# A long convolution followed by a token-mixing layer: GpSimd copies of the input ahead of the first transform's weight loads

## The chip, the cores and the metric

The kernel runs on one core of one Trainium2 chip. The metric is the device time of one execution in microseconds. The engines are named as in the profile: PE is TensorE (PEld its weight loads), DVE is VectorE, ACT is ScalarE, POOL is GpSimd, SP is SyncE, the last of which only issues transfers here.

## The reference

`x` is 8 x 5696 x 128 (batch, token, channel), `h` is 5696 x 128. Two layers follow each other.

```python
# 1: causal long convolution along the tokens, by transforms of twice the length
Xf = np.fft.rfft(x, n=2 * S, axis=1);  Hf = np.fft.rfft(h, n=2 * S, axis=0)
x  = np.fft.irfft(Xf * Hf[None], n=2 * S, axis=1)[:, :S, :]
# 2: phase-aware mixing of the tokens
theta = x @ w_theta                                  # 128 x 128
zr, zi = x * np.cos(theta), x * np.sin(theta)
y = einsum('ts,bsd->btd', w_tok_r, zr) + einsum('ts,bsd->btd', w_tok_i, zi)   # 5696 x 5696 each
u = x + y
out = u + np.maximum(u @ w_ch, 0.0)
```

## The kernel before

The work falls into a transform stage (the first 440 us or so), a stage that computes the phases and writes `zr` and `zi`, and the mixing (two passes of one-level Strassen products over the 5696 x 5696 weights), which takes the rest. The change touches the transform stage alone.

The length 11392 is split as 178 x 64 (`N1` x `N2`). The channels are treated in halves of 64 (`HD`), the batches in pairs, so that there are eight groups `(bp, dh)`: pair `bp`, half `dh`. A group passes four steps:

- **Stage A** (`stage_a`, L185 to L202): the transform of length 178 over the token blocks. The tokens of one batch lie as 89 rows (partitions) of 64; the tile `x16` holds `[89 rows, 2 batches, 64 tokens, 128 channels]` in f16. For each channel one matmul takes as its weights the 2 x 64 columns of that channel and as its moving operand the table `f1_t` of 180 columns. The columns of one channel are 128 elements apart in `x16`, 256 bytes. Four channels make a chunk, in one PSUM tile; 16 chunks make a group. ACT copies each chunk into `a_` (L201). The weights are named by

```python
x16 = x16s[bp].rearrange("p b n d -> p (b n) d")
steps, a_st = stage_a(lambda q: x16[:NB, :, dh * HD + q])
```

- **Stage B** (`stage_b`, `f2`): the transform of length 64 with the twiddles in the weights (L212), ACT's copy out of PSUM (L310), and DVE's two products with the filter's transform, which was computed first and stored in HBM (L312, both inputs in SBUF). Each group's stage B ends with 12 further matmuls (L218), whose output nobody reads.
- **Stage C** (`stage_c`): the way back over 64 points, 16 chunks of 16 matmuls (L328, L329), drained by DVE (L336) and for four of the chunks by ACT (L333, L334).
- **Stage D** (`stage_d`): the way back over 178 points (L351), drained by ACT (L354) and stored in `yt_hbm`.

The order is written out by the function `woven`, which merges lists of steps by given shares of the time. Stage A of group g + 1 is woven into stage C of group g: over the first 35% where g is the first half of a pair (`dh == 0`), over the first 55% otherwise. Stage B of group g + 1 is then woven with stage D of group g. A scheduler beneath the kernel places the instructions on each engine's queue; each queue is worked in order. All transform stages take their PSUM tiles from one ring of four (`psum`).

`x16` has one buffer. `load_x` (L130, sixteen transfers issued by POOL) refills it for the next pair when stage A of the second half has read it. POOL also builds the tables of sines at the beginning: each needs an iota (L150) and a product (L152) by POOL, then work by DVE and ACT. The table `w_table` (used by L212) comes in six parts, `r_table` and `s_table` are woven with stage A of group 0, the three parts of `e_table` with its stage B.

The filter `h` passes the same stage A and `f2` once before, from its own tile `h16`.

Of the kernel before, what the change touches and what calls it, by code (L numbers as in the profile page):

```python
# [12 lines left out]
F16 = mybir.dt.float16  # L13
# [9 lines left out]
def kernel(  # L23
# [10 lines left out]
    nc = tc.nc  # L34
    B, S, D = x.shape
    assert D == 128
    P = 128
# [39 lines left out]
    N2 = 64  # L77
    N1 = NF // N2
    NB = S // N2
    K1 = N1 // 2 + 1  # L80
    CK = 8
    HD = D // 2
# [14 lines left out]
    def psum():  # L97
        return fp.tile([P, 2, 512], F32, tag="ps", name="ps")

    conv, setup, xa, xin, pha = (ExitStack() for _ in range(5))  # L100

    def pool(name, bufs, stack, **kw):
        return stack.enter_context(tc.tile_pool(name=name, bufs=bufs, **kw))

    fa = pool("fft_a", 1, xa)
    fh = pool("fft_h", 4, xa)
    fx = pool("fft_x", 1, xin)
    NE, WB, BT = 9, 6 * 4 * CJ * 64, 7 * 1024
    keep = pool("keep", 1, ctx, side="right")
    fc = pool("fft_c", 1, conv, side="right")  # L110
# [7 lines left out]
    h16 = s1.tile([P, 2, N2, HD], F16)  # L118
# [5 lines left out]
    def load_x(bp):  # L124
        x16 = fx.tile([P, 2, N2, D], F16, tag="x16", name="x16")
        for e in range(2):
            src = x[2 * bp + e]
            for n0 in range(0, N2, 16):
                for p0, p1 in ((0, 80), (80, NB)):
                    nc.gpsimd.dma_start(  # L130
                        x16[p0:p1, e, n0:n0 + 16, :].rearrange("p n d -> p (n d)"),
                        bass.AP(tensor=src.tensor, offset=src.offset + (p0 * N2 + n0) * D,
                                ap=[[N2 * D, p1 - p0], [1, 16 * D]]))
        return x16
# [34 lines left out]
    f1_t = fc.tile([P, 2 * K1], F16)  # L169
# [7 lines left out]
    def w_table(k0):  # L177
        t, k = turns_of([[1, 15], [N1, N2]], k0, lane[:, 0:1], P, NF)
        t3, k3 = (z.rearrange("p (k n) -> p k n", n=N2) for z in (t, k))
        sine(w_t2[:, k0:k0 + 15, :N2], t3, 1)  # L180
        cosine(w_t2[:, k0:k0 + 15, N2:2 * N2], t3, k3)
        nc.vector.tensor_scalar(w_t2[:, k0:k0 + 15, 2 * N2:], w_t2[:, k0:k0 + 15, :N2],
                                -1.0, None, op0=mult)

    def stage_a(lhs, both=False):  # L185

        st = {}

        def chunk(q):
            if q == 0:  # L190
                st["a"] = fa.tile([P, 2 * K1, HD], F16, tag="a", name="a_")
            ps = psum()
            for i in range(4):
                nc.tensor.matmul(ps[:, i // 2, (i % 2) * 2 * K1:(i % 2 + 1) * 2 * K1], lhs(q + i), f1_t[:NB],  # L194
                                 start=True, stop=True)
            a_out = st["a"][:, :, q:q + 4].rearrange("p k (a q) -> p k a q", a=2)
            a_in = ps[:, :, :4 * K1].rearrange("p a (q k) -> p k a q", q=2)
            if both and q % 8:
                nc.vector.tensor_copy(a_out, a_in)
            else:  # L200
                nc.scalar.activation(a_out, a_in, AF.Copy)  # L201
        return [lambda q=q: chunk(q) for q in range(0, HD, 4)], st  # L202
# [19 lines left out]
    def woven(*lists):  # L222

        lists = [l if isinstance(l, tuple) else (l, 0.0, 1.0) for l in lists]
        steps = [(w0 + (i + 0.5) / len(l) * (w1 - w0), n, f)
                 for n, (l, w0, w1) in enumerate(lists) for i, f in enumerate(l)]
        for _, _, f in sorted(steps, key=lambda s: s[:2]):
            f()
# [2 lines left out]
        w_table(k0)  # L231
    nc.vector.tensor_copy(h16[:NB], u_t[:NB, :N2 * D].rearrange("p (n h d) -> p h n d", h=2, d=HD))
    x16s = {0: load_x(0)}
    steps, a_h = stage_a(lambda q: h16[:NB].rearrange("p h n d -> p (h n) d")[:, :, q], True)
    woven(steps, [lambda k0=k0: w_table(k0) for k0 in range(45, K1, 15)])

    hst = [t[:, :6 * D * CK].rearrange("p (c h d k) -> p c h d k", c=6, h=2, k=CK) for t in (u_t, v_t)]
# [56 lines left out]
    def stage_b(a_st, dh):  # L294

        hs_of = {}

        def load(c):
            if c >= NCK:
                return  # L300
            hs = hs_of[c] = fh.tile([P, 2, HD * CK], F16, tag="hs", name="hs")
            for e in range(2):
                nc.sync.dma_start(hs[64 * e:64 * e + 64], hf_hbm[dh, c])

        def chunk(c):
            c0, ck = CHK[c]
            hv = hs_of[c].rearrange("p r (d k) -> p r d k", k=CK)
            ps = f2(a_st, c)
            xs = fs.tile([P, 2, HD, CK], F16, tag="xs", name="xs")
            nc.scalar.activation(xs[:, :, :, :ck], ps, AF.Copy)  # L310
            for r in range(2):
                nc.vector.tensor_tensor(  # L312
                    uv[r][:, :, :, c0:c0 + ck], xs[:, :, :, :ck],
                    hv[:, r:r + 1, :, :ck].to_broadcast([P, 2, HD, ck]), op=mult)
            load(c + LEAD)
        return [lambda c=c: load(c) for c in range(LEAD)], [lambda c=c: chunk(c) for c in range(NCK)]
# [54 lines left out]
    def front(g):  # L371
        if g >= len(groups):
            return [], [], []
        bp, dh = groups[g]
        x16 = x16s[bp].rearrange("p b n d -> p (b n) d")
        steps, a_st = stage_a(lambda q: x16[:NB, :, dh * HD + q])
        return (steps, *stage_b(a_st, dh))

    a0, load0, b0 = front(0)
    woven(a0, [lambda: r_table(0, r_u), lambda: r_table(1, r_v), s_table] + load0)  # L380
    woven(b0, [lambda n0=n0: e_table(n0) for n0 in range(0, EN, 11)])
# [220 lines left out]
    for g, (bp, dh) in enumerate(groups):  # L602
        st = {}
        last = g + 1 == len(groups)
        a_, load_, b_ = front(g + 1)
        if last:
            for _ in range(3):
                steps0.pop(0)()
        now = [with_load(steps0.pop(0), n < 6) for n in range(9)] if last else []
        c_ = stage_c(st, last)  # L610
        if dh == 0 and bp + 1 < B // 2:
            def next_x(bp=bp):
                x16s[bp + 1] = load_x(bp + 1)
            a_ = a_ + [next_x]
        woven((c_, 0.06 if a_ else 0.0, 1.0), (a_, 0.0, 0.35 if dh == 0 else 0.55), now, load_)
        if g + 2 == len(groups):
            xin.close()
            open_phases()
            load_ya0()
        now = [steps0.pop(0) for _ in range(5)] if last else []  # L620
        woven(b_, (stage_d(st, bp, dh, load_ya1 if last else None), 0.0, 1.1 if b_ else 1.0), now)
        if g + 2 == len(groups):
            load_ya1()
            open_ring()
# [56 lines left out]
    bp = cp = wlp = ybp = None  # L681
# [232 lines left out]
    for i, (k, p, tt, j0, s0, nj) in enumerate(stretches):  # L914
# [38 lines left out]
        if tt is None:  # L953
            if p:
                aside(True, False)
            if first_of_pair:
                ps = [mps.tile([P, 512], F32, tag=f"m{q}", name=f"m{q}") for q in ((M1, M7) if p else (M3, M4))]
# [3 lines left out]
            for j in range(nj):  # L961
                jj = j0 + s0 + j
                for r in range(2):
                    b = [x[:, r, :] for x in bts[jj]]
# [182 lines left out]
```

## Time and profile before

| | |
|---|---|
| time, median of 3 runs | 2110.66 us (2108.34 to 2111.68) |
| the profiled execution | span 2116.2 us, 41712 instructions |
| PE matmuls, weight loads | busy 2008.1 us (95%), 1117.7 us (53%) |
| DVE, ACT, POOL | 1598.3 us (76%), 673.9 us (32%), 907.6 us (43%) |
| the chain that ended last | PE 68%, of it L1084 (mixing) 61% of the span |
| granted PE clock, mean | 0.979; 0.70 from 50 to 100 us |

No time of the profiled execution is given but its span, which is 0.26% over the median of the runs; numbers of the profile are set against the span.

A row of the groups names line, engine, operation, output and inputs, shapes and count, then the busy time and the mean of one; behind the second bar stands the idle time of the engine just before these instructions and who ended most of it. A row of the timeline begins with the start and the length in us and merges instructions of the same kind that follow each other. The durations of PE overlap, since matmuls and loads are pipelined; what a matmul costs in a run of them is the distance from start to start.

### The profile page before, as it was taken

How to read it: one execution, taken by the hardware profiler on the slowest of the kernel's cores; microseconds unless marked ns; L12 is line 12 of the kernel's file. 1: busy time of each engine (PE TensorE's matmuls, PEld its weight loads, DVE VectorE, ACT ScalarE, POOL GpSimd, SP SyncE). 2: the span in 40 equal slices, each digit the busy share in tenths (PEclk: the TensorE clock that was granted, in tenths of full speed). 3: DMA queues.
4: the chain of work that ended last, by engine and by line, in shares of the span. 5: the costliest groups of instructions: out<-in, count | busy, mean ns of one | idle time of the engine just before them, and what ended most of it. 6: DMA issues, size and time to landing. Idle time of an engine off the chain costs nothing.

```text
span 2116.2 us, 41712 instructions
## 1 busy us (share of the span) xinstructions
PE 2008.1 (95%) x15873; PEld 1117.7 (53%) x15873; DVE 1598.3 (76%) x2884; ACT 673.9 (32%) x997; POOL 907.6 (43%) x1662
## 2 busy tenths in 40 slices
PE   4888999778999999999999999999999999999998
PEld 3788888654444444444444444444444444444444
DVE  7767776777778888888886755877777777776867
ACT  5778877774332333332310000111111111111111
POOL 5301010227444536354556543445454444545450
PEclk8799999999999999999999999999999999999999
DMA  6457474889989989898999879878888787979693
GB/s 140 98 130 170 117 180 127 216 245 243 178 153 179 176 176 168 170 176 173 174 165 156 142 137 296 128 117 147 140 143 145 134 153 128 156 127 157 124 156 90
DMA packets 408265, 334.97 MB, mean 158 GB/s; under 512 B 85927, under 2 KB 358439, under 8 KB 407079
## 3 DMA queue, kind: packets, MB, share of 16 engines
q0 software_dynamic: 225952, 156.72, 52.5%
q1 hardware_dynamic: 176128, 164.05, 27.3%
q10 hardware_dynamic: 5984, 11.54, 1.6%
q8 instruction: 124, 2.03, 0.4%
q14 instruction: 77, 0.63, 0.1%
HBM read 377.11 MB, written 92.49 MB: 222 GB/s over the span
## 4 chain that ended last, share of the span: by engine, by line
PE 68%; DMA 3%; DVE 3%; POOL 1%; issue 1%; ACT 0%; DVEq 0%; SPq 0%; POOLq 0%; ACTq 0%
PE m L1084 61%; PE m L1005 2%; DMA ring<-in_moe_w_tok_r_dram 1%; DMA b<-z_hbm 1%; POOL ring L509 1%; PE v L801 1%; PE utp L794 1%; DVE c L1091 1%; PE m L1088 1%; DVE b L655 1%; DVE wt L714 1%; DMA ring<-in_moe_w_tok_i_dram 0%; PE theta_ps L396 0%; PE tpz L742 0%; PE m L968 0%
## 5 line engine op out<-in xcount | busy, mean ns | idle before, releaser
L509 POOL DMA_DIRECT2D ring<-in_moe_w_tok_i_dram x720 | 387.9, 546 | 666.7 <-DVE wt L714 587.7
L714 DVE STREAM_TRANSPOSE wt<-ring 128x384 f32<-128x384 f32 (+2 forms) x720 | 360.5, 527 | 123.2 <-PE m L1084 71.3
L509 POOL DMA_DIRECT2D ring<-in_moe_w_tok_r_dram x720 | 386.4, 546 | 149.3 <-DVE wt L714 86.4
L1084 PE MATMUL m<-b,wt 128*128 128x512 bf16 x1640 | 388.3, 379 | 2.0 <-DVE wt L714 1.7
L1084 PEld LDWEIGHTS <-wt 128*128 128x128 bf16 x1804 | 175.8, 98 | 217.6 <-DVE wt L714 6.2
L1091 DVE TENSOR_TENSOR c<-c,m 128x512 f32<-128x512 f32 x412 | 266.9, 674 | 0.4 <-PE m L1084 0.4
L796 ACT ACTIVATE ring<-utp 128x512 bf16<-128x512 bf16 (+1 forms) x86 | 50.9, 592 | 586.2 <-PE utp L794 586.2
L328 PE MATMUL ps<-r_u,u_t 128*128 128x128 f16 x1024 | 128.6, 226 | 10.8 <-ACT red L419 5.6
L329 PE MATMUL ps<-r_v,v_t 128*128 128x128 f16 x1024 | 127.7, 226 | 0.4
L791 ACT ACTIVATE ub<-c 128x512 bf16<-128x512 f32 (+1 forms) x90 | 56.3, 628 | 215.0 <-DMA ring<-in_moe_w_tok_r_dram 123.8
L1005 PE MATMUL m<-b,wt 128*128 128x512 bf16 x480 | 112.9, 385 | 9.1 <-DVE wt L714 4.4
L130 POOL DMA_DIRECT2D x<-in_x_dram x64 | 33.9, 536 | 189.3 <-PE ps L194 177.8
L328 PEld LDWEIGHTS <-u_t 128*128 128x128 f16 x1024 | 104.1, 102 | 9.6 <-DVE u_t L312 6.2
L329 PEld LDWEIGHTS <-v_t 128*128 128x128 f16 x1024 | 103.4, 101 | 5.7 <-issue 3.2
L310 ACT ACTIVATE xs<-ps 128x1024 f16<-128x1024 f32 x96 | 95.9, 1023 | 15.1 <-DVE v_t L312 7.9
L312 DVE TENSOR_TENSOR u_t<-xs,hs 128x1024 f16<-128x1024 f16 x96 | 68.8, 716 | 32.1 <-ACT xs L310 19.7
L1005 PEld LDWEIGHTS <-wt 128*128 128x128 bf16 x528 | 50.8, 99 | 70.8 <-issue 8.7
L194 PE MATMUL ps<-f_t,x 89*128 89x180 f16 x512 | 77.2, 299 | 5.6 <-ACT xs L310 3.9
L212 PEld LDWEIGHTS <-w_t 64*128 64x128 f16 x3240 | 61.2, 102 | 34.8 <-issue 21.7
L398 ACT ACTIVATE red<-theta_ps,magic 128x512 f32<-128x512 f32 (+1 forms) x46 | 31.6, 687 | 133.7 <-PE theta_ps L396 116.0
L194 PEld LDWEIGHTS <-x 89*128 89x128 f16 x512 | 70.3, 241 | 6.6 <-issue 5.9
L744 ACT ACTIVATE ring<-tpz 128x512 bf16<-128x512 bf16 (+1 forms) x46 | 27.5, 597 | 132.6 <-PE tpz L742 108.9
(2914 smaller groups left out, 3916.7 us busy)
## 6 DMA issues: line engine op xcount, KB each, us to landing
ring<-in_moe_w_tok_r_dram POOLq DMA_DIRECT2D x352, 96.0 KB, 4.4
ring<-in_moe_w_tok_i_dram POOLq DMA_DIRECT2D x352, 96.0 KB, 5.0
ring<-in_moe_w_tok_r_dram POOLq DMA_DIRECT2D x352, 80.0 KB, 4.5
ring<-in_moe_w_tok_i_dram POOLq DMA_DIRECT2D x352, 80.0 KB, 3.9
hs<-hf_hbm SPq DMA_DIRECT2D x192, 128.0 KB, 3.2
cp_hbm<-c SPq DMA_DIRECT2D x88, 256.0 KB, 2.6
c<-cp_hbm SPq DMA_DIRECT2D x88, 256.0 KB, 4.4
out_dram<-c SPq DMA_DIRECT2D x88, 256.0 KB, 4.5
```

The source lines that it names most:

```text
L194: nc.tensor.matmul(ps[:, i // 2, (i % 2) * 2 * K1:(i % 2 + 1) * 2 * K1], lhs(q + i), f1_t[:NB], start=True, stop=True)
L212: nc.tensor.matmul(ps[:, e, j * HD:(j + 1) * HD], w_t2[rows, c0 + j, N2 * (1 - ri):N2 * (3 - ri)], a_st["a"][rows, ri * K1 + c0 + j, :], s ...
L310: nc.scalar.activation(xs[:, :, :, :ck], ps, AF.Copy)
L312: nc.vector.tensor_tensor(uv[r][:, :, :, c0:c0 + ck], xs[:, :, :, :ck], hv[:, r:r + 1, :, :ck].to_broadcast([P, 2, HD, ck]), op=mult)
L328: nc.tensor.matmul(o, u_t[:, at:at + P], r_u, start=True, stop=False)
L329: nc.tensor.matmul(o, v_t[:, at:at + P], r_v, start=False, stop=True)
L509: nc.gpsimd.dma_start(wb[32 * i:32 * i + 32, :ng, :nj * 64], bass.AP(tensor=a.tensor, offset=a.offset + row0 * S + p * H + i * QR + j0 * 6 ...
L714: nc.vector.transpose(wt.rearrange("p j t r -> p (j t r)").bitcast(F32).rearrange("p (j g t) -> p g j t", j=TJ, g=4)[:, :ng, :nj], wb[:, : ...
L791: nc.scalar.activation(ub[:m].rearrange("p b d -> p (b d)"), c[:m], AF.Copy)
L1005: nc.tensor.matmul(ms[n // 2 * 2 + h], a[n][:, j, :, r], bts_of[p][jj][n % 2 * 2 + h][:, r, :], start=(n % 2 == 0 and jj == 0 and r == 0), ...
L1084: nc.tensor.matmul(ms[q], a[q][:, j, :, r], bts[jj][q][:, r, :], start=(jj == 0 and r == 0), stop=(jj == NJ - 1 and r == 1 and q not in left))
L1091: nc.vector.tensor_tensor(c, z, ms[q], op=op)
```

## The change

A new pool `fft_xt` of five small buffers, each `[89 rows, 4 channels, 128 columns]` in f16, is opened behind the pool of `x16`. For each chunk of stage A, POOL copies the chunk's four channels out of `x16` into the next buffer, so that the 128 columns of a channel stand side by side; the four weight loads of the chunk then read the buffer. There are 16 copies a group, 128 in all, of 512 elements a row each. `stage_a` now takes a function that is called once a chunk and gives a function of the channel within it. For the filter, the weights are read from `h16` as before. Lines behind L191 move by two, those behind L376 by seven: the matmul is L196, the copy L381, L312 becomes L314.

```diff
@@ pools
     fx = pool("fft_x", 1, xin)
+    fxt = pool("fft_xt", 5, xin)
@@ stage_a, chunk(q)
             ps = psum()
+            cols = lhs(q)
             for i in range(4):
-                nc.tensor.matmul(ps[:, i // 2, (i % 2) * 2 * K1:(i % 2 + 1) * 2 * K1], lhs(q + i), f1_t[:NB],
+                nc.tensor.matmul(ps[:, i // 2, (i % 2) * 2 * K1:(i % 2 + 1) * 2 * K1], cols(i), f1_t[:NB],
                                  start=True, stop=True)
@@ the filter
-    steps, a_h = stage_a(lambda q: h16[:NB].rearrange("p h n d -> p (h n) d")[:, :, q], True)
+    steps, a_h = stage_a(lambda q: lambda i: h16[:NB].rearrange("p h n d -> p (h n) d")[:, :, q + i], True)
@@ front(g)
-        x16 = x16s[bp].rearrange("p b n d -> p (b n) d")
-        steps, a_st = stage_a(lambda q: x16[:NB, :, dh * HD + q])
+        x16 = x16s[bp].rearrange("p b n d -> p d (b n)")
+
+        def cols(q):
+            xt = fxt.tile([P, 4, 2 * N2], F16, tag="xt", name="xt")
+            nc.gpsimd.tensor_copy(xt[:NB], x16[:NB, dh * HD + q:dh * HD + q + 4])
+            return lambda i: xt[:NB, i]
+        steps, a_st = stage_a(cols)
         return (steps, *stage_b(a_st, dh))
```

## The prediction

> **What bounds the kernel now.** I read the page first (shares, the forty slices, the costliest groups), then the windows of 50 us, then the timeline of the transform stage, which is the only place the edit touches.
>
> ```profile
> span 2116.2 us, 41712 instructions
> L194 PE MATMUL ps<-f_t,x 89*128 89x180 f16 x512 | 77.2, 299 | 5.6 <-ACT xs L310 3.9
> L194 PEld LDWEIGHTS <-x 89*128 89x128 f16 x512 | 70.3, 241 | 6.6 <-issue 5.9
> L329 PEld LDWEIGHTS <-v_t 128*128 128x128 f16 x1024 | 103.4, 101 | 5.7 <-issue 3.2
> L1084 PE MATMUL m<-b,wt 128*128 128x512 bf16 x1640 | 388.3, 379 | 2.0 <-DVE wt L714 1.7
> ```
>
> 61% of the chain that ended last is L1084, the mixing after 520 us, where no line of the edit works. The first transform (L194) runs only before 361 us. A load of its weights takes 241 ns, one of equally many columns lying side by side (L329) takes 101 ns. So the most that can be won is a part of 77 us, 3.6% of the span.
>
> ```profile
> 177.87 1.57 PEld L194 LDWEIGHTS <-x 89*128 89x128 f16 x12
> 177.93 1.67 PE L194 MATMUL ps<-f_t,x 89*128 89x180 f16 x12
> 178.66 4.64 ACT L201 ACTIVATE a__3378<-ps 128x720 f16<-128x720 f32 x6 [0.36 <-PE ps L194]
> 187.42 4.13 POOL L130 DMA_DIRECT2D x<-in_x_dram  x8 [75.13 <-PE ps L194]
> ```
>
> Twelve loads in 1.57 us are 131 ns each; the 180 moving columns behind one need less: L1084 streams 24 x 512 columns in 5.18 us, 0.421 ns a column, so 76 ns. TensorE is held by the weights. GpSimd is idle there (75 us in one piece). Between 100 and 350 us ScalarE is busy 79% and VectorE 73%, so neither is far behind TensorE.
>
> ```profile
> L152 POOL TENSOR_SCALAR turn<-whole,lane 128x960 f32<-128x960 f32 x6 | 6.8, 1139 | 0.5
> L152 POOL TENSOR_SCALAR turn<-whole,lane 128x1 f32<-128x1 f32 x1 | 0.3, 266 | 0.1
> L507 POOL COPY ring<-zz 1x1 bf16<-1x1 bf16 x6 | 1.1, 177 | 13.2 <-DVE zz L432 13.2
> 53.18 5.40 POOL L150 IOTA whole<- 90x979 f32 x2 [2.51 <-DVE sgn L290]
> 58.67 5.05 POOL L152 TENSOR_SCALAR turn<-whole,lane 90x979 f32<-90x979 f32 x2
> 68.87 3.23 POOL L152 TENSOR_SCALAR turn<-whole,lane 90x979 f32<-90x979 f32 x1
> 81.74 0.68 DVE L312 TENSOR_TENSOR v_t<-xs,hs 128x1024 f16<-128x1024 f16 x1
> 83.43 2.06 DVE L312 TENSOR_TENSOR u_t<-xs,hs 128x1024 f16<-128x1024 f16 x1
> 83.50 1.75 PEld L194 LDWEIGHTS <-x 89*128 89x128 f16 x13
> ```
>
> The first three rows price GpSimd. The next two show the same GpSimd work, 1.0 us (iota) and 1.14 us (L152) when alone, at 2.7 and 2.5 us while L194 loads its strided weights; the sixth shows it at 3.23 us beside a run of L312. The last three: L312 takes 0.68 us alone and 2.06 us beside strided loads. Both kinds of neighbour cost something, and the edit removes one and brings more of the other.
>
> **The change, part by part.** *The loads.* The 512 loads come to about the 101 ns of L329, whose pairs follow each other every 55 ns; the pair is then set by its columns, 76 instead of 131 ns. One chunk (four pairs) falls from 0.53 to 0.30 us. What that is worth depends on the weave. In the steps that prepare the second half of a batch pair (four: groups 1, 3, 5, 7) three chunks share TensorE with one chunk of stage C (16 matmuls in 0.86 us): 2.45 us a round. ScalarE drains a chunk each 0.65 us, so the round falls to 1.95 at best: 0.5 x 4 rounds = 2.0 us. In the three steps for the next pair (2, 4, 6) a round is two chunks and one of C, 1.9 us, held by TensorE: 12 chunks x 0.22 = 2.7 us. Both also get back the L312 that strided loads slow, about 1 us at each step's start, where stage C waits for it. Without any other limit: -3.0 and -3.7 us, in all -12.0 and -11.1.
>
> *The copies.* 128 copies of 512 elements, read 256 bytes apart. No row shows such a read on GpSimd. From below: 0.18 us (the 1x1 copy) plus 512 x 0.91 ns (the slope of the two L152 rows) is 0.64. From above, undisturbed: TensorE's pitch goes up 131 / 55 = 2.4 times for the same pattern; applied to the slope, 0.18 + 1.12 = 1.30 us. Beside L312, the row of 3.23 against 1.14 makes 2.8 times 0.64, 1.8 us. I take 1.30, since the only rows with this stride are those of L194, and keep 0.64 and 1.8 for the range.
>
> [...]
>
> *The pace.* Five buffers let five copies run ahead. The sixth waits until chunk 0 has left TensorE, 0.6 us after the step begins, and the last chunk follows its copy by 0.4: a step can't be shorter than 0.6 + 11 x 1.30 + 0.4 = 15.3 us. By the rows of L194, first start to last end, the steps now take 16.2, 14.1, 15.6 and 17.3 us (groups 1, 3, 5, 7) and 18.4, 18.2 and 16.3 (2, 4, 6). All the floors above lie under 15.3, so GpSimd sets the length: -0.9 + 1.2 - 0.3 - 2.0 = -2.0, and -3.1 - 2.9 - 1.0 = -7.0. TensorE works in a fixed order, so stage C behind shifts by as much, and so does all after it; I know of no slack before the mixing that would eat it.
>
> *Group 0.* Here the copies stand in a queue with work. In the built order five copies come ahead of the last table's iota, seven ahead of the first L152 of the e table, three ahead of the second, and six (one of group 0, five of group 1) ahead of the third iota. Five copies from about 35.6 us (x has landed) end at 42.1; the iota now starts at 40.66, and its table releases TensorE: +1.5. Then stage A of group 0, which is held by its matmuls at half clock (granted 0.5 from 49.4 to 63.0) and so gains nothing: the two iotas, rid of the strided loads, end near 55.2, and 11 copies and two L152 of 1.1 us end at 71.7; the last chunk is drained at 72.9, where it is now at 65.1: +7.8. The first L312 stands behind that. The third e table waits behind five more copies: +1.2. Together +10.5.
>
> *The port.* For the odd pairs x lands near 207 us, and the five copies ahead fall among L312s (207 to 219). In the trace a GpSimd read waited 2 us for such a run to pause; a copy that starts in a pause holds VectorE up in turn. VectorE has 2 to 3 us of pauses there and five copies ask for 6.5: I put 1.5 us on each of three steps and 0.5 on the others, whose sixth copy meets the last L312s: +6.5. Bounds: 0 (the copies fit the pauses) and 15.
>
> [...]
>
> Nothing else moves: TensorE, ScalarE and SyncE keep their order, VectorE changes places of a few instructions. The loads of x, queued behind the copies, wait for the last copy instead of the last matmul, which comes no later. Costed at nothing: the 75 us of idle GpSimd cover it; without that cover the load, 20 us from first issue to landing, would stand ahead of each odd pair's copies.
>
> Sum: 10.5 - 2.0 - 7.0 + 6.5 = +8.0 us on the profiled 2116.2 (2124.2). The median of the runs is 2110.7, 0.26% under the span; the same 8.0 gives 2118.7.
>
> **The rivals.** *A quick copy (faster).* At 0.9 us the pace is 10.9 us, under all floors: -12.0 - 11.1, group 0 costs 3.8 and the port 4.5: -14.8, so 2095.9. For it: 0.64 is what GpSimd does on adjacent data. Against it: the stride. The sign turns at 1.22 us a copy (at 1.2 us the same sum gives -1). *Copies stretched in use.* At 1.6 us the pace is 18.6: +11.2 and +2.9, group 0 +15, port +7: +36, 2147. For it: the rows of 2.5 to 3.2 us. Against it: VectorE's L336 in these steps reads PSUM and one table, not two buffers. *A draw*, at 1.15 to 1.26 us a copy: within 4 us of 2110.7. That the loads don't become quick I hold unlikely: a buffer's channel is 128 adjacent f16, as in v_t.
>
> **How the numbers follow.** The forecast (1.26 to 1.5 us a copy) has 0.37, stretched copies 0.13, a quick copy 0.38, a draw 0.12. A difference under 0.2% (4.2 us) can't be told from none here. So slower 0.50, same 0.12, faster 0.38. The range runs from 2091 (a copy at its lower bound, 0.64 us: the floors, -23.1, group 0 +0.5 and port +3) to 2138 (a copy of 1.5 us: +6.8 - 0.4 + 14 + 7), which leaves out the stretched copies' far end; the forecast's own is 2115 to 2138.
>
> **What would show it.** Right: copies of L381 at 1.2 to 1.5 us; loads of L196 near 100 ns; L196's chunks from the sixth on waiting for GpSimd, 1.3 us apart; steps of 15 us; group 0's last chunk near 73 us; no L314 over 1 us beside loads. Wrong: copies under 1.1 us with TensorE waiting for ScalarE, or the mixing beginning earlier than now.

## The result, and the profile after

| | before | after |
|---|---|---|
| time, median of 4 runs | 2109.5 us (2107.35 to 2111.68) | 2128.93 us (2127.12 to 2129.64) |
| ratio, 95% interval | | 1.0078 (1.0063 to 1.0094) |
| span of the profiled execution | 2116.2 us | 2127.5 us |
| first start of a stage C, of the last stage C | 87.9, 392.1 us | 103.2, 408.6 us |
| first matmul of the mixing stage (L1005, after: L1012) | 456.8 us | 468.0 us |

The kernel became slower: by the ratio 0.8%, or 16.5 us (13 to 20), while these two medians lie 19.4 us apart. All of it lies before the mixing: from the first matmul of L1005 to the end of the span the two profiles take 1659.4 and 1659.5 us. The last stage C begins 16.5 us later, which fits the ratio. That the mixing is only 11.2 us late comes from the profile of before: its last stage C, interleaved with the phases, took 34.6 us, while after's took 30.7 and those of all the experiments below 28.5 to 32.5. So that one execution lost some 4 us in a place that no copy touches; why is open. Below, the delay at the last stage C is set against the ratio.

The rows of after's page that answer to those of before:

```profile
span 2127.5 us, 41747 instructions
...
L381 POOL COPY xt<-x 89x512 f16<-89x512 f16 x128 | 149.7, 1215 | 134.2 <-PE ps L196 112.2
...
L330 PEld LDWEIGHTS <-u_t 128*128 128x128 f16 x1024 | 103.8, 101 | 16.1 <-DVE u_t L314 14.5
...
L312 ACT ACTIVATE xs<-ps 128x1024 f16<-128x1024 f32 x96 | 92.0, 979 | 23.2 <-DVE v_t L314 15.4
L314 DVE TENSOR_TENSOR u_t<-xs,hs 128x1024 f16<-128x1024 f16 x96 | 77.0, 803 | 28.0 <-ACT xs L312 19.5
...
L314 DVE TENSOR_TENSOR v_t<-xs,hs 128x1024 f16<-128x1024 f16 x96 | 79.7, 830 | 0.0
...
L196 PE MATMUL ps<-f_t,xt 89*128 89x180 f16 x512 | 57.4, 260 | 12.7 <-POOL xt L381 9.3
```

The views of after's lines L381 and L196 add the spread, as least, median and greatest duration in ns, then the first and last start:

```profile
L381 POOL COPY xt<-x x128: 1032/1068/2097, 37.3 to 375.0; 89x512 f16<-89x512 f16 x128
```

```profile
L196 PEld LDWEIGHTS <-xt x512: 95/98/153, 58.0 to 377.7; 89*128 89x128 f16 x171
```

The change did to TensorE what it says: a load takes 98 ns where it took 238 (medians). A copy takes 1.07 us as a median, but 1.215 as a mean: the 52 that overlapped a VectorE instruction with two inputs in SBUF (the products of L314, or the table work at the beginning) took 1.44 us on average. The products show the other half: a full one (1024 elements) takes 0.69 us alone, and the 34 that overlapped copies took 1.31 on average. What that looks like is in the timeline of after, where x for the last pair has just landed while stage B is under way:

```profile
307.09 0.69 DVE L314 TENSOR_TENSOR u_t<-xs,hs 128x1024 f16<-128x1024 f16 x1
307.20 7.42 POOL L381 COPY xt<-x 89x512 f16<-89x512 f16 x5 [6.71 <-DMA x<-in_x_dram]
307.69 1.60 DVE L314 TENSOR_TENSOR v_t<-xs,hs 128x1024 f16<-128x1024 f16 x1
...
309.22 1.55 DVE L314 TENSOR_TENSOR u_t<-xs,hs 128x1024 f16<-128x1024 f16 x1
...
310.69 1.55 DVE L314 TENSOR_TENSOR v_t<-xs,hs 128x1024 f16<-128x1024 f16 x1
...
312.35 1.02 ACT L312 ACTIVATE xs<-ps 128x1024 f16<-128x1024 f32 x1 [1.91 <-DVE v_t L314]
...
313.42 1.88 PE L214 MATMUL ps<-a__5564,w_t 64*128 64x64 f16 x64 [1.97 <-ACT xs L312]
...
315.10 0.68 DVE L314 TENSOR_TENSOR u_t<-xs,hs 128x1024 f16<-128x1024 f16 x1
```

Five copies begin at 307.20 and end at 314.62, 1.48 us each. For just as long every product takes 1.53 to 1.60 us, and the first one behind the last copy takes 0.68 again. In these 7.4 us copies and products begin by turns, each kind about 1.5 us apart (copies at 307.20, 308.66 and 310.16, products at 307.69, 309.22 and 310.69). ScalarE then waits for the product (1.91 us) and TensorE for ScalarE (1.97 us). This stage B lasts 19.2 us, where it lasted 16.1.

### The profile page after: what moved, and what is told of

It is laid out like the page before. It is cut to its first block, busy times and chain, and to the rows that moved or that the text cites. A ratio compares the mean times of both kernels' runs of the same rounds, so it can differ in the third digit from the quotient of the medians.

```text
span 2127.5 us, 41747 instructions
## 1 busy us (share of the span) xinstructions
PE 1979.3 (93%) x15695; PEld 1096.0 (52%) x15873; DVE 1614.1 (76%) x2884; ACT 660.6 (31%) x997; POOL 1050.2 (49%) x1790
## 4 chain that ended last, share of the span: by engine, by line
PE 64%; DVE 4%; DMA 2%; issue 1%; POOL 0%; ACT 0%; DVEq 0%; POOLq 0%
PE m L1091 59%; DVE c L1098 1%; DMA ring<-in_moe_w_tok_r_dram 1%; PE v L808 1%; PE utp L801 1%; PE m L1095 1%; DVE b L662 1%; DVE wt L721 1%; DMA ring<-in_moe_w_tok_i_dram 0%; PE m L975 0%; PE m L977 0%; PE theta_ps L403 0%; PE tpz L749 0%; POOL ring L516 0%; PE m L1012 0%
## 5 line engine op out<-in xcount | busy, mean ns | idle before, releaser
L1091 PE MATMUL m<-b,wt 128*128 128x512 bf16 x1599 | 384.5, 379 | 4.2 <-DVE wt L721 1.7
L381 POOL COPY xt<-x 89x512 f16<-89x512 f16 x128 | 149.7, 1215 | 134.2 <-PE ps L196 112.2
L331 PE MATMUL ps<-r_v,v_t 128*128 128x128 f16 x1024 | 128.0, 226 | 4.4 <-DVE v_t L314 4.3
L1012 PE MATMUL m<-b,wt 128*128 128x512 bf16 x466 | 110.6, 382 | 10.5 <-DMA b<-z_hbm 4.7
L330 PEld LDWEIGHTS <-u_t 128*128 128x128 f16 x1024 | 103.8, 101 | 16.1 <-DVE u_t L314 14.5
L331 PEld LDWEIGHTS <-v_t 128*128 128x128 f16 x1024 | 103.7, 101 | 12.7 <-issue 7.1
L312 ACT ACTIVATE xs<-ps 128x1024 f16<-128x1024 f32 x96 | 92.0, 979 | 23.2 <-DVE v_t L314 15.4
L314 DVE TENSOR_TENSOR u_t<-xs,hs 128x1024 f16<-128x1024 f16 x96 | 77.0, 803 | 28.0 <-ACT xs L312 19.5
L1012 PEld LDWEIGHTS <-wt 128*128 128x128 bf16 x528 | 50.8, 98 | 71.4 <-issue 9.8
L314 DVE TENSOR_TENSOR v_t<-xs,hs 128x1024 f16<-128x1024 f16 x96 | 79.7, 830 | 0.0
L196 PE MATMUL ps<-f_t,xt 89*128 89x180 f16 x512 | 57.4, 260 | 12.7 <-POOL xt L381 9.3
```

Of the source, the lines that this page charges most:

```text
L314: nc.vector.tensor_tensor(uv[r][:, :, :, c0:c0 + ck], xs[:, :, :, :ck], hv[:, r:r + 1, :, :ck].to_broadcast([P, 2, HD, ck]), op=mult)
L330: nc.tensor.matmul(o, u_t[:, at:at + P], r_u, start=True, stop=False)
L331: nc.tensor.matmul(o, v_t[:, at:at + P], r_v, start=False, stop=True)
L381: nc.gpsimd.tensor_copy(xt[:NB], x16[:NB, dh * HD + q:dh * HD + q + 4])
L1012: nc.tensor.matmul(ms[n // 2 * 2 + h], a[n][:, j, :, r], bts_of[p][jj][n % 2 * 2 + h][:, r, :], start=(n % 2 == 0 and jj == 0 and r == 0), ...
L1091: nc.tensor.matmul(ms[q], a[q][:, j, :, r], bts[jj][q][:, r, :], start=(jj == 0 and r == 0), stop=(jj == NJ - 1 and r == 1 and q not in left))
```

## The experiments

All differ from the kernel after only in where stage A's weights come from, save the last two. Groups 0 and 1 "direct" means that they load from `x16` with its 256-byte steps, as before. Differences in us are between a kernel's median and that of the kernel before, run beside it.

**1. What the quick loads alone are worth.**

```diff
-    fxt = pool("fft_xt", 5, xin)
...
+        flat = x16s[bp].rearrange("p b n d -> p (b n d)")
...
+            if g < 2:
+                return lambda i: x16[:NB, dh * HD + q + i]
-            xt = fxt.tile([P, 4, 2 * N2], F16, tag="xt", name="xt")
-            nc.gpsimd.tensor_copy(xt[:NB], x16[:NB, dh * HD + q:dh * HD + q + 4])
-            return lambda i: xt[:NB, i]
+            at = (dh * HD + q) * 2 * N2
+            return lambda i: flat[:NB, at + i * 2 * N2:at + (i + 1) * 2 * N2]
```

> Groups 0 and 1 load their weights from x with the stride, as before. Groups 2 to 7 load 128 adjacent columns of x, with no copy ahead of them (they are other columns than the reference asks for, so this run only prices quick loads without copies). Theory A (the loads are worth what the prediction said, and what is lost is lost to the copies): the floors of the prediction, -3.7 us in each of three even-numbered groups and -3.0 in each of three odd-numbered ones, about -20 us against the kernel before, 2090; no L312 product over 1 us in groups 2 to 7. Theory B (quick loads are worth little, since ScalarE and VectorE are close behind TensorE): within 5 us of the kernel before.

Measured: 2091.15 against 2112.18 us, ratio 0.9901 (0.9874 to 0.9928), 21 us faster. The groups of this kernel's profile from 200 to 400 us:

```profile
L313 DVE TENSOR_TENSOR u_t<-xs,hs 128x1024 f16<-128x1024 f16 (+1 forms) x54 | 35.8, 664 | 18.5 <-ACT xs L311 10.8 <-DMA hs<-hf_hbm 6.8
...
L195 PEld LDWEIGHTS <-x 89*128 89x128 f16 x256 | 19.9, 97 | 2.3 <-issue 2.1
```

The loads are worth what the prediction's floors said: 20.1 us for the six steps that prepare groups 2 to 7 (a step being a stage A woven with the stage C before it; 23.1 for all seven), against 21 here. TensorE's granted clock, which the floors left out, may have a part in this: between the first and the last start of a stage C it was halved for 33 us in before and for 14 here. No product in those groups takes over 0.9 us any more, where before has ten of 1.01 to 1.73 us, so the slow products beside strided loads were caused by these loads.

**2. The same six groups with the copies.**

```diff
+            if g < 2:
+                return lambda i: x16[:NB, dh * HD + q + i]
```

> The changed kernel, but groups 0 and 1 load from x with the stride and make no copies, so that GpSimd's table work stands alone in its queue again. Theory A1 (most of the loss is made in group 0, where the copies stand among the table work): stage C of group 0 begins at 88 us again, and the time falls by 14 to 17 us against the changed kernel, to 2112 to 2115. Theory A2 (the loss is spread over all groups, at each step's start and where x lands): it falls by a quarter of what was lost, to about 2124.

Measured: 2122.04 against 2112.18 us, ratio 1.0049 (1.0032 to 1.0067). So the loss does not sit in group 0 alone; six groups of copies turn a gain of 21 us into a loss of 10. The copies are as before, 1.07 us as a median, in the view of the copy's line:

```profile
L383 POOL COPY xt<-x x96: 1037/1070/1584, 119.5 to 366.6; 89x512 f16<-89x512 f16 x96
```

Of the products 42 overlap copies: 30 full ones take 1.28 us on average, and ten of the 12 short ones (256 elements) 1.23 to 1.26. Together they are 26 us longer than alone, at 0.69 and 0.39 us.

**3. The same GpSimd time without the reads.**

```diff
+            if g < 2:
+                return lambda i: x16[:NB, dh * HD + q + i]
...
-            nc.gpsimd.tensor_copy(xt[:NB], x16[:NB, dh * HD + q:dh * HD + q + 4])
+            nc.gpsimd.tensor_copy(xt[:NB, :, :1], x16[:NB, dh * HD + q:dh * HD + q + 4, :1])
+            nc.gpsimd.memset(xt[:NB], 0.01)
+            nc.gpsimd.memset(xt[:NB, :2], 0.01)
```

> As the run with groups 0 and 1 direct, but in groups 2 to 7 each copy of 512 elements is replaced by GpSimd work of the same length that reads almost nothing: a copy of 4 elements and memsets of 512 and 256 into the buffer (so the weights are a constant). The pace, the waits and the quick loads stay; the reads go. Theory P (VectorE's two-input products and GpSimd's reads exclude each other): no product over 0.8 us in groups 2 to 7, and 5 to 12 us faster than the run with groups 0 and 1 direct. Theory Q (GpSimd's pace of about 1.1 us a chunk is what limits): no faster than that run, within 3 us. Theory R (any GpSimd access to SBUF stretches VectorE): the products stay at 1.2 to 1.6 us, and no gain.

Measured: 2096.54 against 2112.18 us, ratio 0.9926 (0.9906 to 0.9946). That is 25.5 us less than experiment 2, where 5 to 12 were expected: the direction was right, the size twice too small at least. The timeline of this kernel shows the same place as a step's beginning in after, whose timeline stands below it:

```profile
168.41 0.52 POOL L384 MEMSET xt<- 89x512 f16 x1
...
168.80 0.39 DVE L314 TENSOR_TENSOR u_t<-xs,hs 128x256 f16<-128x256 f16 x1
168.87 0.39 POOL L383 COPY xt<-x 89x4 f16<-89x4 f16 x1
169.11 0.39 DVE L314 TENSOR_TENSOR v_t<-xs,hs 128x256 f16<-128x256 f16 x1
...
169.25 0.10 PEld L330 LDWEIGHTS <-u_t 128*128 128x128 f16 x1 [0.18 <-DVE u_t L314]
```

```profile
185.26 5.18 POOL L381 COPY xt<-x 89x512 f16<-89x512 f16 x4 [20.89 <-PE ps L196]
...
185.65 1.56 DVE L314 TENSOR_TENSOR v_t<-xs,hs 128x1024 f16<-128x1024 f16 x1
...
187.14 1.22 DVE L314 TENSOR_TENSOR u_t<-xs,hs 128x256 f16<-128x256 f16 x1
188.28 1.24 DVE L314 TENSOR_TENSOR v_t<-xs,hs 128x256 f16<-128x256 f16 x1
188.41 0.10 PEld L330 LDWEIGHTS <-u_t 128*128 128x128 f16 x1 [2.12 <-DVE u_t L314]
...
189.57 0.10 PEld L331 LDWEIGHTS <-v_t 128*128 128x128 f16 x1 [1.05 <-DVE v_t L314]
```

Stage C needs the last, short products (256 elements). With copies beside them they take 1.22 and 1.24 us instead of 0.39 each, and TensorE stands 2.12 and 1.05 us, with a single matmul between. With the memsets it waits 0.18. From 100 to 400 us such waits of stage C's loads for products come to 16.5 us in experiment 2 and to 5.0 here, and the stages B of groups 1 to 7 are 5.3 us longer in experiment 2; for the rest see TensorE's clock below. GpSimd has as much to do per chunk in both kernels: 0.20 + 0.52 + 0.31 = 1.03 us against 1.06. So GpSimd's pace costs at most the 5.4 us between this kernel and experiment 1, and its reads, with all that follows from them, cost 25. The full products beside memsets, which only write, take 0.69 us here, those beside copies, which also read, 1.28 in experiment 2.

**4. Copies that read adjacent elements.**

```diff
+        flat = x16s[bp].rearrange("p b n d -> p (b n d)")
...
+            if g < 2:
+                return lambda i: x16[:NB, dh * HD + q + i]
...
-            nc.gpsimd.tensor_copy(xt[:NB], x16[:NB, dh * HD + q:dh * HD + q + 4])
+            at = (dh * HD + q) * 2 * N2
+            nc.gpsimd.tensor_copy(xt[:NB], flat[:NB, at:at + 8 * N2].rearrange("p (c n) -> p c n", c=4))
```

> As the run with groups 0 and 1 direct, but the copies of groups 2 to 7 read 512 adjacent elements of x (other ones than the reference asks for). It prices the stride of GpSimd's read. If the stride costs: a copy falls from 1.06 us to about 0.64, and the time by 3 to 6 us against the run with groups 0 and 1 direct, most of it at the steps' starts. If not: the copy stays at 1.0 to 1.1 us and the time within 2 us.

Measured: 2105.12 against 2112.18 us, ratio 0.9963 (0.9951 to 0.9974). The view of the copy's line:

```profile
L385 POOL COPY xt<-x x96: 603/610/1173, 113.0 to 346.1; 89x512 f16<-89x512 f16 x96
```

The 256-byte step of the read costs 0.46 us of 1.07. The shorter copy is worth 17 us where 3 to 6 were expected, since it also leaves the products alone sooner: 29 of them overlap copies and are 8.5 us longer in all, instead of 26.

**5. Copies in group 0 alone.**

```diff
+            if g:
+                return lambda i: x16[:NB, dh * HD + q + i]
```

> Only group 0 loads through copies; groups 1 to 7 load from x with the stride, as before. Prices the place of the copies among GpSimd's table work. If group 0's delay is passed on whole: stage C of group 0 begins 12 to 15 us later than in the kernel before, and the time is 12 to 15 us over it, 2122 to 2126. If later stages absorb a part: stage C of group 0 as late, but the time only 5 to 8 us over the kernel before.

Measured: 2124.33 against 2113.47 us, ratio 1.0041 (1.0022 to 1.0060), 10.9 us slower. The first stage C starts at 100.1 us, 12.2 later than before, and the delay is passed on nearly whole. Both in this kernel and in after the table work and the copies of group 0 take turns on GpSimd; the timeline of after:

```profile
37.27 7.54 POOL L381 COPY xt<-x 89x512 f16<-89x512 f16 x5 [1.59 <-DMA x<-in_x_dram]
...
41.92 1.98 DVE L157 SCALAR_TENSOR_TENSOR turn<-whole,turn 128x960 f32<-128x960 f32 x1
...
44.77 0.98 POOL L151 IOTA whole<- 128x960 f32 x1
...
56.94 2.20 POOL L151 IOTA whole<- 90x979 f32 x2 [2.50 <-DVE sgn L292]
...
59.10 7.00 POOL L381 COPY xt<-x 89x512 f16<-89x512 f16 x7
...
67.34 4.56 POOL L381 COPY xt<-x 89x512 f16<-89x512 f16 x3
...
72.00 1.91 POOL L153 TENSOR_SCALAR turn<-whole,lane 90x979 f32<-90x979 f32 x1
...
73.97 9.35 POOL L381 COPY xt<-x 89x512 f16<-89x512 f16 x6
...
75.55 0.78 PE L196 MATMUL ps<-f_t,xt 89*128 89x180 f16 x4 [2.81 <-POOL xt L381]
...
76.37 0.77 ACT L203 ACTIVATE a__725<-ps 128x720 f16<-128x720 f32 x1 [2.82 <-PE ps L196]
```

The first five copies take 1.51 us each beside VectorE's table work, and the last iota starts at 44.77 instead of 40.66. Then stage A of group 0 goes at GpSimd's pace: its last chunk is drained at 77.1, it was at 65.1.

**6. A step of 128 bytes instead of 256, no copies.** One run.

```diff
-    fxt = pool("fft_xt", 5, xin)
...
+        flat = x16s[bp].rearrange("p b n d -> p (b n d)")
...
-            xt = fxt.tile([P, 4, 2 * N2], F16, tag="xt", name="xt")
-            nc.gpsimd.tensor_copy(xt[:NB], x16[:NB, dh * HD + q:dh * HD + q + 4])
-            return lambda i: xt[:NB, i]
+            if g < 2:
+                return lambda i: x16[:NB, dh * HD + q + i]
+            return lambda i: flat.rearrange("p (h n d) -> p h n d", h=2, d=HD)[:NB, dh, :, q + i]
```

> Groups 2 to 7 load 128 columns of x that lie 128 bytes apart instead of 256, with no copies (other columns than the reference asks for). If the load's price goes with the stride: about 90 ns a pair and most of the gain of adjacent columns, 2095. If any stride over one line costs the same: loads of 230 to 240 ns and the time of the kernel before, 2105 to 2115.

Measured: 2098.1 us, beside a median of 2113.47. The groups of this kernel from 200 to 360 us:

```profile
L195 PEld LDWEIGHTS <-x 89*128 89x128 f16 x256 | 26.6, 185 | 1.3 <-issue 1.3
```

Half the step brings about 15 of the 21 us, though a load still takes 185 ns.

**7. Copies kept away from the products.** Group 0 direct; the first five chunks direct in groups 1, 2, 4 and 6. Ahead of the first copy of a group GpSimd copies one element of the last product (`v_t`), and so waits until VectorE is through.

```diff
+        gate = []
...
+            k = q // 4
+            if g == 0 or (k < 5 and (dh == 0 or g == 1)) or k in ():
+                return lambda i: x16[:NB, dh * HD + q + i]
...
-            nc.gpsimd.tensor_copy(xt[:NB], x16[:NB, dh * HD + q:dh * HD + q + 4])
+            if k >= 5 and not gate:
+                gate.append(nc.gpsimd.tensor_copy(xt[96:97, 0, :1], uv[1][96:97, 1, HD - 1, K1 - 1:]).ins)
+            with tc.issue_after(gate[0]) if gate else ExitStack():
+                nc.gpsimd.tensor_copy(xt[:NB], x16[:NB, dh * HD + q:dh * HD + q + 4])
```

> Copies only where VectorE has no two-input product to do. Group 0 loads from x with the stride. Groups 1, 2, 4 and 6 load their first five chunks with the stride too, so nothing is copied ahead among the products of stage B. In every group a copy of one element of v_t, which waits for the last product of stage B, stands on GpSimd's queue ahead of the copy for chunk 5. If the exclusion between products and GpSimd's reads is the loss: products over 0.8 us only beside strided loads (at most three a group), each even-numbered group 1 to 2 us and each odd-numbered one 2 us over the run with adjacent loads and no copies, so 2097 to 2104, faster than the kernel before by 0.3 to 0.6%. If the pace of GpSimd limits as well (the copies now begin 2 to 3 us later in each step): 2110 or more.

Measured: 2107.08 against 2113.47 us, ratio 0.9969 (0.9957 to 0.9981). That is between the two forecasts. No product overlaps a copy; nine overlap strided loads and are 6 us longer together. With the copies begun later, chunks now follow each other at 0.8 to 1.2 us in places, and the loads of stage A wait 18.1 us for copies in all: here GpSimd does set part of the pace.

**8. The same, with chunks 8 and 12 direct too**, so that GpSimd has 78 copies to make instead of 92 (after has 128). The edit against experiment 7:

```diff
-            if g == 0 or (k < 5 and (dh == 0 or g == 1)) or k in ():
+            if g == 0 or (k < 5 and (dh == 0 or g == 1)) or k in (8, 12):
```

> As the gated run, and chunks 8 and 12 of each group load with the stride, which takes two of eleven copies off GpSimd's pace. If the pace limits the gated run, 1 to 2 us faster a step, 7 to 12 us in all; if not, the strided chunks cost 0.2 us each, 2 to 3 us slower.

Measured: 2101.95 against 2113.47 us, ratio 0.9945 (0.9928 to 0.9961), 5 us better than experiment 7, where 7 to 12 were expected, and faster than both kernels. The loads now wait 9.7 us for copies. The timeline of this kernel at the start of a step:

```profile
171.54 0.39 DVE L314 TENSOR_TENSOR u_t<-xs,hs 128x256 f16<-128x256 f16 x1
171.84 0.39 DVE L314 TENSOR_TENSOR v_t<-xs,hs 128x256 f16<-128x256 f16 x1
171.98 0.10 PEld L330 LDWEIGHTS <-u_t 128*128 128x128 f16 x1 [0.18 <-DVE u_t L314]
...
172.38 0.19 POOL L386 COPY xt<-v_t 1x1 f16<-1x1 f16 x1 [23.93 <-DVE v_t L314]
...
172.63 10.11 POOL L388 COPY xt<-x 89x512 f16<-89x512 f16 x9
...
173.75 0.27 PEld L196 LDWEIGHTS <-xt 89*128 89x128 f16 x4 [0.35 <-POOL xt L388]
```

GpSimd waits for `v_t`, the short products stay at 0.39 us, and nine copies pass at 1.12 us each.

**9 and 10. Shorter steps made by the transfers.** The kernel before, with x laid out in `x16` by halves (128-byte steps) or quarters (64-byte steps) of the channels. No copies; the transfers of x write pieces of 128 or 64 bytes. The edit for the halves:

```diff
-        x16 = fx.tile([P, 2, N2, D], F16, tag="x16", name="x16")
+        x16 = fx.tile([P, 2, 2, N2, HD], F16, tag="x16", name="x16")
...
-                    nc.gpsimd.dma_start(
-                        x16[p0:p1, e, n0:n0 + 16, :].rearrange("p n d -> p (n d)"),
...
+                    for h in range(2):
+                        nc.gpsimd.dma_start(
+                            x16[p0:p1, h, e, n0:n0 + 32, :],
...
```

> The kernel before, with x16 laid out by halves of 64 channels, so that a channel's columns lie 128 bytes apart instead of 256; the transfers of x write pieces of 128 bytes and no engine copies anything. If the stride alone sets the load's price, as the look at half the stride suggests (loads of 185 ns, 15 us less): 2096 to 2102, with groups 0 and 1 gaining as well. If the short pieces slow the transfers of x (20 us now, with 10 us to spare before the next step): x lands after the next step has begun, and the gain is lost, 2110 or more.

> The same by quarters of 32 channels: 64 bytes apart, pieces of 64 bytes. If the load's price falls with the stride again: loads of 110 to 150 ns and 3 to 6 us less than by halves. If the transfers' pieces decide: slower than by halves, x landing up to twice as late.

Measured: 2123.17 against 2113.01 us for the halves, ratio 1.0053 (1.0031 to 1.0076), and 2207.84 for the quarters, ratio 1.0447 (1.0419 to 1.0475). The DMA view's row of the queue that carries x, in before, in the halves and in the quarters (packets, MB, share of the 16 engines):

```profile
q0 software_dynamic: 225952, 156.72, 52.5%
```

```profile
q0 software_dynamic: 321184, 156.75, 62.7%
```

```profile
q0 software_dynamic: 420512, 156.78, 75.0%
```

The same bytes in more packets. In the halves a load takes 183 ns and stage A of groups 1 to 7 shrinks to 11.6 to 13.5 us (from 14.1 to 18.4), but transfers of x land after 10.3 us instead of 6.8 (medians), and every stage B beside them grows, from 18.0, 16.8 and 16.1 to about 25 to 27 us. A row of its timeline names one such wait, for the filter's transfer:

```profile
211.76 0.69 DVE L313 TENSOR_TENSOR u_t<-xs,hs 128x1024 f16<-128x1024 f16 x1 [3.42 <-DMA hs<-hf_hbm]
```

In the quarters stage A itself waits for x, 48.1 us in three waits in the view of the waits:

```profile
PE ps L195 <- DMA x<-in_x_dram: 48.1, 3, 17.7
```

So the gain of experiment 6 can't be had from the transfers in this way.

## Why the prediction was right, and where it was not

The verdict, slower, was right, and 2128.9 us lies in the range and in the forecast's own. It is 10 us above the number, and the reasoning holds only in part. That the verdict came out right is partly luck: the copy was taken too slow, which lengthened the predicted steps for a reason that is not there, and the price of its reads was taken too low, and the two errors pulled against each other. Taken at the last stage C, the terms compare thus. Stage A, B and C lengths are read from the first start to the last end of the matmuls of each group; the steps are the lengths of stage C, and the pauses run from the end of a stage B to the first matmul of the stage C behind it.

| term | predicted, us | measured, us |
|---|---|---|
| group 0 | +10.5 | +15.2 (first stage C) |
| odd-numbered steps (four) | -2.0 | +1.4 |
| even-numbered steps (three) | -7.0 | -6.5 |
| pauses ahead of stage C | in the steps | +0.4 |
| the prediction's "port", in stage B | +6.5 | +6.0 (all of stage B's change) |
| sum | +8.0 | +16.5 |

**The copy: mis-sized.** I took 1.30 us, reasoning by TensorE's ratio for the same stride; undisturbed it is 1.06 (within the bounds of 0.64 and 1.8). This miss matters: put 1.06 into the prediction's own formulas and the pace is 0.6 + 11 x 1.06 + 0.4 = 12.7 us, below or near all floors. The steps then give -10.3 and -11.0; group 0 and the port, scaled between the values given for 0.9 and 1.30 us, cost 6.5 and 5.3. The sum is -9.5, faster. So the turning point "1.22 us a copy" was wrong; the copy was quick and the kernel slower all the same.

**The pace: the step that failed.** "GpSimd sets the length" is not what the profile shows. Experiment 3 keeps GpSimd's time per chunk and is within 5.4 us of no copies at all. Inside the steps of after, ScalarE drains most chunks 0.65 to 0.91 us apart, less than one copy: GpSimd has the pause at the step's start to run ahead in. L196's matmuls wait 9.3 us for copies in all, and all of it in group 0; behind it every chunk's copy is done at least 0.24 us before the chunk's first load. Experiment 7, with the copies begun later, has a pace in part.

**The port: the place and the size.** No run shows a port; what they show is a full product of 1.31 us on average beside copies in after, of 0.69 alone. Under that name I charged 6.5 us, for copies that fall among stage B's products; stage B did grow by 6.0. What I missed is that each step begins with copies beside the last products, for which stage C waits: the pause of 2.12 + 1.05 us shown above. Of the floors' 23.1 us the steps and the pauses ahead of them kept only 4.7. By experiments 2 and 3 the reads of six groups cost 25 us, far above the bound of 15 that I gave. "No L314 over 1 us beside loads" holds for the loads (experiment 1), but the copies put slow products of their own in the place of those.

**TensorE's clock: a term that the sum did not have.** In after each of the four steps that prepare an odd-numbered group begins with TensorE at half its clock: the granted clock was 0.50 from 102.2 to 109.1, 187.6 to 194.4, 276.3 to 283.1 and 365.1 to 371.9 us. Stage C's matmuls then start 107 ns apart, as in these rows of after; experiment 3's start 56 ns apart at the same place:

```profile
190.72 0.31 PE L330 MATMUL ps<-r_u,u_t 128*128 128x128 f16 x1
190.83 0.31 PE L331 MATMUL ps<-r_v,v_t 128*128 128x128 f16 x1
```

The view by windows gives the busy time of each engine and behind it the granted clock (1.00 in before, 0.93 in after); 150 to 200 us, before and then after:

```profile
150.00:200.00 50.00, 45.84 (x984) 42.95 (x982) 36.72 (x41) 38.95 (x53) 8.20 (x16) 1.00 0.59 139
150.00:200.00 50.00, 44.39 (x928) 41.44 (x925) 36.21 (x40) 39.84 (x55) 27.17 (x27) 0.93 0.48 130
```

Between the first and the last start of a stage C the clock was halved for 33 us in before and 47 in after, for 14, 60, 17 and 34 in experiments 1 to 4, and for 19 and 14 in experiments 7 and 8. In after stage C's first load of these four steps had waited 4.06, 2.12, 3.58 and 2.95 us for its product, against 0.32 to 1.21 at any step's start in before. In experiments 1, 3, 7 and 8, where no copy of 512 elements runs beside the last products, the steps that prepare groups 3, 5 and 7 have no half clock at all; in after and experiment 2 each of them has. So the pauses seem to be paid twice, once as waiting and once in the slow matmuls behind them. That is argued from the profiles, not shown: no run holds the clock fixed, and in before, also without copies, these three steps have 0, 3.4 and 4.8 us of half clock behind waits of 0.47, 0.88 and 0.60 us. Half of 43 us, 22, is the most that the clock can account for in the 25 us between experiments 2 and 3. It would also explain why the odd-numbered steps did not shrink although none of their loads waits for a copy: the clock was halved for 24 us of them in after, for 14 in before.

**Group 0: right in kind, short in size.** The start of stage A came 4.6 us later where +1.5 was said, since the five copies took 1.51 us each and slowed VectorE's table work (1.98 us for 1.16). Stage A itself grew by 8.6 (predicted 7.8), and 2.0 us came behind it (1.2). The remark that it "is held by its matmuls at half clock (granted 0.5 from 49.4 to 63.0)" misread the profile of before: the granted clock was 1.00 from 52.6 to 59.4 us, and the pairs there follow each other every 138 ns, where the twelve at 177.87 us take 131. So quick loads could have gained something here; the pace of the copies hid it. Of the 15.2 us, 3.0 come from group 1's copies in the same queue: experiment 5, without these, is 12.2 us late at the first stage C, and 10.9 in time.

**The loads: right.** 98 ns as said, the floors met by experiment 1 (with whatever part the clock has in it), and the three even-numbered steps, whose pause at the start is short (L331 waits 1.02 us in the last of them), gained 6.5 of the 7.0 us predicted.

**The rivals.** "A quick copy" came true in its premise and failed in its sign, for the reads. "Copies stretched in use" is nearer to what happened: 52 copies at 1.44 us on average, up to 2.1. But it, too, would have had GpSimd's pace lengthen the steps. Its argument against, that VectorE in these steps reads PSUM and one table, was right for the steps' body (in after L338 takes 1.22 us with or without a copy beside it, and a copy beside L338 alone 1.06) and overlooked their beginning.

## What to carry to other kernels

Price a helper engine's copy by what it slows, not by its own length or its engine's idle time: here a copy of 1.06 us on an idle GpSimd went with products of 1.31 us on average instead of 0.69 (full ones, in after), and those products were what the next stage waited for. Look behind a pause of the fast engine, too: behind after's four longest, 2.12 to 4.06 us, TensorE's matmuls started 107 ns apart instead of 56, at a granted clock of 0.50; whether the pause brought that is not shown. Look at what the neighbour does at the very moment when the copies run, above all at the start of a stage, when buffers are free and all copies come at once; holding them until the last product was done, leaving out the stage whose queue they delayed, and loading some chunks directly (78 copies instead of 128) turned the edit from 0.8% slower to 0.55% faster. And where a queue's work stands on the way to the first result, nothing should be put ahead of it.

## What the runs showed of the hardware

- A load of 128 columns of weights took 97 ns from adjacent columns (experiment 1), 183 to 185 at a step of 128 bytes (experiments 9 and 6; the filter's, in before, 173) and 241 at 256 (before). Beside loads with the step of 256, 12 products of 0.69 us took 1.0 to 2.1 us in before; with adjacent loads and no copies (experiment 1) none of those in groups 2 to 7 took over 0.9.
- GpSimd's copy of 512 f16 a row took 0.61 us from adjacent elements (experiment 4) and 1.07 from elements 256 bytes apart (experiment 2), as medians.
- Five of GpSimd's copies beside VectorE's products of two SBUF operands took 1.48 us each and the products about 1.55 in after, from 307.20 to 314.62 us, instead of 1.06 and 0.69. Beside GpSimd's memsets the products took 0.69 (experiment 3).
- TensorE's granted clock was 0.50 for 6.8 us at the start of each of after's four steps for odd-numbered groups, and matmuls started 107 ns apart there instead of 56; without copies of 512 elements beside the last products (experiments 1, 3, 7 and 8) the steps for groups 3, 5 and 7 had none of it, and in before, also without copies, 0, 3.4 and 4.8 us.
- A transfer of x cut into 128-byte pieces landed after 10.3 us (experiment 9, median) instead of 6.8 (before), and the longest wait of a product for the filter's transfer, on another queue, grew from 1.3 to 3.9 us.
